# Loads of an attention decode kernel put in another order, and its MLP tail cut into chunks

## Chip, cores and metric

The kernel runs on one core of one Trainium2 chip. The metric is the device time of one execution in microseconds (us). Times in the profile count from the first instruction; the span in the profile is about 1.8 us shorter than the device time of the same run (731.0 and 732.81).

## The reference

The reference is one decode step of a transformer block for 8 sequences, with one new token each: adaptive layer norm, grouped-query attention over a cache of 8192 keys, and an MLP with a squared relu.

```python
mod = (silu(c) @ w_mod).reshape(8, 6, 1, -1)        # sa, ca, ga, sb, cb, gb
h = layernorm(x) * (1 + ca) + sa
q = (h @ wq)                                        # 32 query heads of 128
scores = einsum(q, k_cache) * 128 ** -0.5           # k_cache, v_cache: 8 x 8 heads x 8192 x 128, bf16
o = einsum(softmax(scores), v_cache)
x = x + ga * (o @ wo)
h = layernorm(x) * (1 + cb) + sb
r = relu(h @ w1 + b1)                               # 512 -> 1792
x = x + gb * ((r * r) @ w2 + b2)
```

The caches are 268 MB (2 x 8 x 8 x 8192 x 128 elements of 2 bytes), the weights about 15 MB. So the work is mostly reading.

## The kernel before

PE is the matmul engine, DVE, ACT and POOL are the vector, scalar and general engines, SP is the engine that issues the transfers, and SBUF is the memory on the core. There are 64 units, one for each sequence and KV head: a K load of 2 MB (2,097,152 bytes) and a V load of the same size. Unit u of K is transposed on PE, copied by DVE and multiplied with the queries. After the eight units of a sequence comes its softmax, and then its eight PV products, which are interleaved with the K units of the next sequence. Phase p therefore holds the K units of sequence p and the PV units of sequence p - 1. K has 4 slots in SBUF and V has 4. All loads are issued by one engine, SP, in program order, each after a wait for its slot.

```python
def k_unit(b, kvh, ...):
    ...
    if kn_use[ks] >= 1:
        W(SPq, S_ktfree[gbp], cntp)               # K slot: last transposed group copied out
    SPq(dma_start(Knat(ks), A_k_cache[b, kvh]...))
    ...
def v_unit(b, kvh):
    u = b * KVH + kvh
    vs = u % NVS
    ...
    if v_use[vs] >= 1:
        W(SPq, S_vfree[vs], v_use[vs])            # V slot: PV of unit u - 4 done
    SPq(dma_start(Vslot(vs), A_v_cache[b, kvh]...))
    ...                                            # 64 matmuls with 4 columns each
for ph in range(B + 1):
    for k in range(KVH):
        ...
        if ph < B:  k_unit(ph, k, ...)
        if ph >= 1:
            if ph == B and k == 4:
                epi_weights_a()                    # w1, w2 into K slots
                epi_weights_b()                    # wo into the transposed-K region, one transfer
            v_unit(ph - 1, k)
...
# the end: one wo product (32 matmuls), layer norm, then on [8, 1792] as a whole:
# w1 product -> + b1 (DVE) -> relu (ACT) -> square (DVE) -> 14 transposes -> copy -> w2 product -> + b2 (DVE)
```

## Time and profile before

| | before |
|---|---|
| device time, median of the first 4 runs | 732.29 us |
| mean load rate from 110 to 600 us | 425 GB/s |
| last V load usable on PE | 692.09 us |
| attention output (PV) done | about 694.0 us |
| wo product done | 703.9 us |
| output transfer issued | 729.31 us |

The page of the profile gives the span in 40 equal slices of 18.3 us. Each digit is a busy share in tenths (9 is 90% or more). DMA is the mean busy share of the core's 16 DMA engines, and the last line the rate in GB/s.

```profile
...
PE   3699898889889898989998988889888897640464
...
DMA  8999999999999999999999999999999999799600
GB/s 345 421 407 381 427 425 427 427 423 426 426 425 424 425 424 424 426 425 424 423 427 426 424 425 426 425 425 427 424 424 426 424 424 417 298 361 369 292 0 0
...
```

The rate is flat at 425 GB/s from slice 5 on. It dips in slice 4 (381), is low in slices 35 to 38, and is nothing in the last two. The table of windows shows the same in longer stretches: busy us of each engine (with its number of instructions), the granted clock, the DMA share and the rate.

```profile
...
core 0: us, PE busy (x) PEld busy (x) DVE busy (x) ACT busy (x) POOL busy (x), PEclk, DMA share, GB/s
50.00:65.00 15.00, 13.66 (x318) 12.78 (x315) 13.70 (x17) 0.00 (x0) 0.00 (x0) 1.00 0.95 354
110.00:600.00 490.00, 430.54 (x9524) 415.39 (x9521) 285.11 (x334) 65.39 (x390) 0.00 (x0) 0.79 1.01 425
616.00:640.00 24.00, 17.81 (x415) 16.79 (x416) 12.78 (x18) 2.10 (x13) 0.00 (x0) 0.78 0.83 326
640.00:694.00 54.00, 14.49 (x507) 13.91 (x504) 2.13 (x3) 8.79 (x54) 0.00 (x0) 0.50 0.90 342
...
```

In the long middle part the DMA engines are always busy (1.01) and PE is not (430.54 of 490 us). Share and rate are means over sixteen engines.

The list of waits (engine and line waiting, what it waited for; us in all, times, longest) shows what PE waits for at the end.

```profile
...
PE ps_ot L454 <- DMA Vb<-in_A_v_cache_dram: 33.5, 4, 24.5
...
```

The timeline (start, duration, engine, line, operation, output <- input, count) shows the end of the kernel.

```profile
...
653.21 15.28 SPq L442 DMA_DIRECT2D Vb<-in_A_v_cache_dram  x4
...
677.44 1.87 PE L454 MATMUL ps_ot<-PexpT,Vb 128*128 128x4 bf16 x64 [24.50 <-DMA Vb<-in_A_v_cache_dram]
...
692.09 1.87 PE L454 MATMUL ps_ot<-PexpT,Vb 128*128 128x4 bf16 x64 [2.99 <-DMA Vb<-in_A_v_cache_dram]
694.06 0.42 DVE L554 TENSOR_TENSOR OT_sb<-ps_ot,RB_sb 128x256 bf16<-128x256 f32 x1 [42.74 <-PE ps_ot L454]
...
694.54 9.35 PE L564 MATMUL ps_st<-KK,OT_sb 128*8 128x512 bf16 x32 [0.59 <-DVE OT_sb L554]
...
703.93 0.68 DVE L573 TENSOR_TENSOR ST_sb<-ps_st,mod_sb 8x512 f32<-8x512 f32 x1 [9.44 <-PE ps_st L564]
...
710.02 4.56 PE L610 MATMUL ps_kt<-KK,h2T 128*8 128x512 bf16 x16 [0.33 <-ACT h2T L591]
...
714.62 2.21 DVE L621 TENSOR_TENSOR KK<-ps_kt,b_sb 8x512 f32<-8x512 f32 x4 [5.25 <-PE ps_kt L610]
716.86 1.70 ACT L624 ACTIVATE KK<-KK 8x1792 f32<-8x1792 f32 x1 [6.89 <-DVE KK L621]
718.58 2.01 DVE L626 TENSOR_TENSOR Vb<-KK 8x1792 bf16<-8x1792 f32 x1 [1.76 <-ACT KK L624]
...
721.52 5.62 PE L648 MATMUL ps_st<-KK,r2T 128*8 128x512 bf16 x14 [0.34 <-ACT r2T L639]
...
729.31 0.31 SPq L665 DMA_DIRECT2D out_dram<-Vb  x1
```

The last four V loads (653.21, SP) reach PE from 677.44 to 692.09. Then follows a chain in which nothing overlaps and nothing is loaded: OT, the wo product 9.35, layer norm until 710.02, w1 product 4.56, bias 2.21, relu 1.70, square 2.01, w2 product 5.62. From the last V to the end it takes 39 us.

### The profile page before, as it was taken

Reading aid. Unit: us, or ns where it says so; the run is one execution under the profiler, and the core shown is the slowest. Engines: PE = TensorE matmul, PEld = TensorE weight load, DVE = VectorE, ACT = ScalarE, POOL = GpSimd, SP = SyncE. Lnnn points to the kernel's source line nnn. Section 1 sums busy time; section 2 is a strip of 40 time slices with the busy share of each in tenths; the row PEclk is TensorE's granted clock in tenths of the full one; section 3 lists DMA queues with packets and bytes.
Section 4 is the critical chain, followed back from the end, with each engine's and each line's share of the span. In section 5 each row is a group of like instructions: output and inputs, shape, how many; then the busy total and the mean of one; then the engine's idle time right before and its main releaser. Section 6 shows DMA issues by size and latency. Waiting matters only on the chain.

```text
span 731.0 us, 26450 instructions
## 1 busy us (share of the span) xinstructions
PE 581.6 (80%) x12560; PEld 540.9 (74%) x12560; DVE 384.7 (53%) x459; ACT 96.7 (13%) x535; POOL 2.0 (0%) x11
## 2 busy tenths in 40 slices
PE   3699898889889898989998988889888897640464
PEld 1688797879888798889987888789887897630321
DVE  0489665556565665556665554665555664510023
ACT  2000410005000500050003200050005000050001
POOL 0000000000000000000000000000000000000000
PEclk9799878768797877777778787876888878855567
DMA  8999999999999999999999999999999999799600
GB/s 345 421 407 381 427 425 427 427 423 426 426 425 424 425 424 424 426 425 424 423 427 426 424 425 426 425 425 427 424 424 426 424 424 417 298 361 369 292 0 0
DMA packets 26123, 285.39 MB, mean 390 GB/s; under 512 B 2168, under 2 KB 8088, under 8 KB 9120
## 3 DMA queue, kind: packets, MB, share of 16 engines
q1 hardware_dynamic: 26016, 283.71, 92.9%
q8 instruction: 98, 1.61, 0.9%
q14 instruction: 9, 0.07, 0.0%
HBM read 283.69 MB, written 0.01 MB: 388 GB/s over the span
## 4 chain that ended last, share of the span: by engine, by line
issue 94%; PE 3%; DMA 1%; DVE 1%; ACT 0%; SPq 0%; POOLq 0%; POOL 0%; ACTq 0%
DMA KK<-in_w_mod_dram 1%; PE ps_st L648 1%; PE ps_kt L610 1%; PE ps_kt L264 1%; PE ps_st L264 0%; DVE KK L621 0%; DVE Vb L626 0%; ACT KK L624 0%; DVE st L280 0%; DVE ST_sb L292 0%; DVE ST_sb L659 0%; DVE Vb L294 0%; DVE ST_sb L657 0%; DVE Vb L661 0%; POOLq L668 0%
## 5 line engine op out<-in xcount | busy, mean ns | idle before, releaser
L385 DVE COPY KK<-ps_kt 128x2048 bf16<-128x2048 bf16 x256 | 311.9, 1223 | 223.2 <-PE ps_kt L378 217.2
L378 PE MATMUL ps_kt<-ident,KK 128*128 128x128 bf16 x4096 | 350.1, 254 | 27.0 <-DMA KK<-in_A_k_cache_dram 17.1
L378 PEld LDWEIGHTS ps_kt<-ident,KK 128*128 128x128 bf16 x4096 | 303.0, 116 | 31.8 <-DMA KK<-in_A_k_cache_dram 18.7
L401 PE MATMUL ps_st<-QT,KK 128*128 128x4 bf16 x4096 | 146.7, 166 | 20.5 <-issue 12.1
L401 PEld LDWEIGHTS ps_st<-QT,KK 128*128 128x128 bf16 x4096 | 135.3, 100 | 34.7 <-DVE KK L385 20.0
L454 PE MATMUL ps_ot<-PexpT,Vb 128*128 128x4 bf16 x4096 | 119.6, 168 | 50.5 <-DMA Vb<-in_A_v_cache_dram 33.5
L454 PEld LDWEIGHTS ps_ot<-PexpT,Vb 128*128 128x128 bf16 x4096 | 114.2, 98 | 51.8 <-DMA Vb<-in_A_v_cache_dram 33.9
L490 ACT ACTIVATE PexpT<-ST_sb,NB_sb 128x64 bf16<-128x64 f32 x256 | 85.0, 333 | 0.2
L480 ACT COPY NB_sb<-ps_m 128x32 f32<-128x32 f32 x8 | 1.5, 185 | 529.4 <-PE ps_m L477 529.4
L490 ACT ACTIVATION_READ_ACCUMULATOR PexpT<-ST_sb,NB_sb 128x1 f32 x256 | 47.8, 187 | 0.0
L415 DVE COPY ST_sb<-ps_st 128x256 f32<-128x256 f32 x64 | 26.7, 417 | 16.8 <-PE ps_st L401 15.7
L417 DVE TENSOR_REDUCE pmax<-ST_sb 128x4 f32<-128x256 f32 x64 | 26.9, 420 | 2.2
L554 DVE TENSOR_TENSOR OT_sb<-ps_ot,RB_sb 128x256 bf16<-128x256 f32 x1 | 0.4, 425 | 42.7 <-PE ps_ot L454 42.7
L564 PE MATMUL ps_st<-KK,OT_sb 128*8 128x512 bf16 x32 | 9.3, 463 | 0.6 <-DVE OT_sb L554 0.6
L468 PE MATMUL ps_m<-ident,pmax_bf 128*32 128x128 bf16 x8 | 2.1, 264 | 9.5 <-DVE pmax_bf L465 9.5
L264 PE MATMUL ps_st<-KK,scT 128*8 128x512 bf16 x8 | 3.6, 628 | 7.6 <-DMA KK<-in_w_mod_dram 7.6
L280 DVE BATCH_NORM_STATS2 st<-x_sb 8x6 f32<-8x512 bf16 x1 | 0.7, 682 | 16.2 <-ACT mod_sb L271 16.2
L468 PEld LDWEIGHTS ps_m<-ident,pmax_bf 128*32 128x32 bf16 x8 | 0.8, 96 | 10.2 <-DVE pmax_bf L465 10.2
L591 ACT CAST h2T<-ps_m 128x32 bf16<-128x32 f32 x1 | 0.2, 185 | 61.0 <-PE ps_m L586 61.0
L564 PEld LDWEIGHTS ps_st<-KK,OT_sb 128*8 128x8 bf16 x32 | 3.3, 104 | 6.3 <-issue 3.2
L264 PEld LDWEIGHTS ps_st<-KK,scT 128*8 128x8 bf16 x8 | 0.9, 119 | 9.4 <-issue 9.4
L498 DVE CAST psr_hi<-psr 128x32 bf16<-128x32 f32 x8 | 1.4, 173 | 11.3 <-ACT PexpT L490 11.3
(67 smaller groups left out, 71.2 us busy)
## 6 DMA issues: line engine op xcount, KB each, us to landing
KK<-in_A_k_cache_dram SPq DMA_DIRECT2D x64, 2048.0 KB, 27.6
Vb<-in_A_v_cache_dram SPq DMA_DIRECT2D x64, 2048.0 KB, 31.0
Vb<-in_A_wq_dram SPq DMA_DIRECT2D x1, 4096.0 KB, 24.0
KK<-in_A_wo_dram SPq DMA_DIRECT2D x1, 4096.0 KB, 36.1
KK<-in_B_w_dram SPq DMA_DIRECT2D x2, 1792.0 KB, 22.5
KK<-in_w_mod_dram SPq DMA_DIRECT2D x1, 3072.0 KB, 10.2
b_sb<-in_B_b_dram SPq DMA_DIRECT2D x1, 28.0 KB
x_sb<-in_A_x_dram SPq DMA_DIRECT2D x1, 8.0 KB
```

Of the source, the lines that this page charges most:

```text
L264: mm = t.matmul(mod_bank(j), scT[:, kt, :], wmod_v[:, kt, j * CH:(j + 1) * CH], start=(kt == 0), stop=(kt == KT - 1))
L378: mm = t.matmul(kt_ps_tile(gb, j), Knat(ks)[:, tt, :], ident[:, :], is_transpose=True, start=True, stop=True)
L385: DVEq(lambda v, gb=gb, kts=kts, g=g: v.tensor_copy(KTs_grp(kts, g), kt_ps_grp(gb)).then_inc(S_ktfree[gb].h, 1))
L401: mm = t.matmul(ps_st[:, stb * 512 + tt * REP:stb * 512 + (tt + 1) * REP], KTs_tile(kts, tt), QT[:, b, kvh * REP:(kvh + 1) * REP], start=T ...
L415: DVEq(lambda v: v.tensor_copy(ST_sb[:, kvh, :, :], src).then_inc(P_dve.h, 1))
L417: DVEq(lambda v: v.tensor_reduce(pmax[:, kvh * REP:(kvh + 1) * REP], ST_sb[:, kvh, :, :], AX.X, ALU.max).then_inc(S_stfree[stb].h, 1))
L454: mm = t.matmul(ps_ot[:, col:col + REP], Vt(vs, tt), rhs, start=(tt == 0), stop=(tt == NT - 1))
L468: PEq(lambda t: t.matmul(ps_m[0:R, 0:P], pmax_bf[:, :], ident[:, :], start=True, stop=True).then_inc(P_pe.h, 1))
L490: ACTq(lambda a, kvh=kvh, h=h, r=r: a.activation(PexpT[:, pslot, kvh, h, :], ST_sb[:, kvh, h, :], ACT.Exp, bias=NB_sb[:, r:r + 1], scale=1 ...
L564: mm = t.matmul(AO_PS, lhsT, wo_v[:, Hh, :], start=(Hh == 0), stop=(Hh == HQ - 1))
L610: mm = t.matmul(mlp_bank(j, wdt), h2T[:, kt, :], w1_v[:, kt, n0:n0 + wdt], start=(kt == 0), stop=(kt == KT - 1))
L648: mm = t.matmul(Y_PS, r2T[:, kt, :], w2_v[:, kt, :], start=(kt == 0), stop=(kt == FT - 1))
```

## The change

The intent is to keep the load queue full and to overlap the end. It has five parts:

1. V0 to V3 are issued during phase 0, where until now only K was loaded.
2. The last four V units (60 to 63) go into K slots, which are free by then, so their loads need not wait for PV.
3. wo, w1 and w2 are loaded after all V, wo in eight pieces with a semaphore each; w1 and w2 go into V slots.
4. The biases are loaded as one row and added by a one-row matmul with ones at the end of each sum; relu, square, transposes and w2 product run in four chunks.
5. (1 + scale) of both layer norms is computed in the prologue.

```diff
+        def v_issue_early(u):                       # called for u = 0..3 after K4..K7 of phase 0
+            ...
+            SPq(dma_start(Vslot(u), A_v_cache[0, u]...))
         def v_unit(b, kvh):
+            tail = (b == B - 1) and (kvh >= KVH - NTAIL)
+            if not tail:
+                ...                                  # as before, or already issued early
+            else:
+                ks = u % NKN
+                W(SPq, S_ktfree[gbk], cntk)          # K slot of the same unit
+                SPq(dma_start(Knat(ks), A_v_cache[b, kvh]...))
...
-                    if ph == B and k == min(NVS, KVH - 1):
-                        epi_weights_a()
-                        epi_weights_b()
                     v_unit(ph - 1, k)
+        epi_weights()                               # wo in 8 pieces, then w1, w2
...
-        W(PEq, S_ldwo, ldwo)
+        for i in range(NWO):
+            W(PEq, S_ldwo[i], ldwo[i])
+            ...                                      # 4 of the 32 matmuls
...
+        for j, (n0, wdt) in enumerate(mlp_chunks):  # 512, 512, 512, 256 columns
+                for kt in range(KT):
+                    t.matmul(mlp_bank(j, wdt), h2T[:, kt, :], w1_v[:, kt, n0:n0 + wdt], start=(kt == 0), stop=False)
+                t.matmul(mlp_bank(j, wdt), ones_row, b1_sb[0:1, n0:n0 + wdt], start=False, stop=True)
...
+        for j, (n0, wdt) in enumerate(mlp_chunks):  # relu -> square -> transposes -> copy -> w2 product
```

## The prediction

> **What bounds the kernel now.** The memory stream does, until the epilogue. In the table of windows, 110 to 600 us runs at 425 GB/s with a DMA share of 1.01, while PE is 88% busy and waits little. One in-order SP queue loads everything (283.7 MB; 667 us at 425 GB/s), so slower stretches are time lost. The DMA packets in short windows show three:
>
> 1. 50 to 65 us: 355 GB/s. Phase 0 loads only K, into 4 slots, at 6.0 us of compute a unit; a 2 MB load takes 4.9 us. Loss about 2.6 us.
> 2. 616 to 640 us: about 320 GB/s, 5.7 us lost. The last V loads are let out one by one, every 10 us, as PV frees a slot (604.3 ... 634.9 us).
> 3. 635 to 692 us: w1, w2 and wo (7.9 MB, mostly 1 KB packets, 350 GB/s) go ahead of the last four V loads, whose issue waits for PV and then stands 13.8 us behind wo's descriptors. PE idles 24.5 us; the last V is used at 692.1.
>
> Then 37 us without any load: wo product 9.4, layer norm 6.1 to the next matmul, w1 product 4.6, bias 2.2, relu 1.7, square 2.0, transposes and copy 0.9, w2 product 5.6, three vector operations 2.1, output 1.7 (timeline).
>
> **What the change does.** V0 to V3 are issued during phase 0, which fills loss 1: -2.6 us, carried to the end by the memory bound. The last four V go into K slots, free since 633 us, so they are issued straight behind V59; wo (8 pieces with a semaphore each), w1 and w2 follow. Loss 2 stays: V56 to V59 still wait for PV in the same in-order queue. [...] the V waits hold back everything behind them.
>
> Tail, in the old clock, from V59's issue at 634.9:
> - data from 636.4; five V of 2.1 MB at 425 GB/s: until 661.1, last used about 663, PV done about 665 (was 694.0);
> - wo 4.2 MB at 350 GB/s: until 673.1, landed about 674.8; its matmuls keep pace with the pieces, done about 676 (was 703.9). The product is hidden, its load exposed;
> - layer norm less 0.45: w1 product starts 681.7. w1 lands about 679.5, w2 about 684.6: just in time;
> - w1 product with 4 bias rows (20 matmuls): 5.5, until 687.2;
> - relu, square, transposes and w2 in four chunks, partly overlapped: estimate 7.2 instead of 12.6, until 694.4 (6.2 to 8.3 by PE clock: 512-column matmuls show 0.21 and 0.43 us);
> - two vector operations 1.45, output 1.7: 697.5.
>
> Less the 2.6 of loss 1: a span of 695 (was 731.0), so a time of 696 us. By parts: tail order -27.8, MLP overlap and biases -5.3, phase 0 -2.6, layer norm -0.45. All is critical.
>
> **Prediction:** 696 us, 690 to 702 in 8 of 10. Faster by over 2%: 0.97; within 2%: 0.02; slower: 0.01.
>
> **What would show it:** 425 GB/s through 50 to 65 us; the dip at 615 to 640 still there; no PE gap of 24 us before a PV unit; last PV about 662, wo matmuls in groups waiting for DMA until 673, w1 product starting about 679 without a DMA wait.
>
> **What would make it wrong:** wo pieces slower than 350 GB/s; w1 or w2 landing late (a DMA wait before the w1 product); V early delaying K of phase 0 so that PE work is lost later; chunk hand-overs dearer than 0.1 us each.

What the trace shows is the order of issue: SP waited 79.3 us for PV (56 times, longest 10.3), V56 to V59 were issued at 604.3, 614.9, 625.1 and 635.0, and w1, w2 and wo only after them, at 635.3, 635.8 and 636.4. "Data from 636.4" can be seen in the packets: there the 16 KB packets under way at one time go from 8 to 14. The 13.8 us are the length of V60's issue (653.21 to 667.0); that wo's descriptors held it up is my reading.

## The result

| | before | after |
|---|---|---|
| device time, median (range) | 732.77 us (731.78 to 734.58, 12 runs) | 707.04 us (704.64 to 709.41, 9 runs) |
| ratio of the mean times, 95% interval | | 0.9644 (0.9628 to 0.966) |
| span of the profiled run | 731.0 us | 705.9 us |

A ratio here is the mean time of one kernel's fast runs over that of the other's of the same rounds, so it is not quite the ratio of the medians quoted. The kernel became 3.6% faster, clear of noise. The forecast of 696 us, with 690 to 702 as its range, was missed by 11 us: about 26 us were gained where 36 were expected.

The slices of the page after (17.6 us each):

```profile
...
PE   3699699888889889888988898997988798893667
...
DMA  8999999999999999999999999999999999989990
GB/s 345 426 425 426 425 426 424 425 424 424 397 425 428 422 419 421 426 426 425 424 426 422 424 425 423 424 426 425 425 424 423 427 424 425 403 329 371 397 336 4
...
```

The dip of slice 4 is gone (426), and PE works through the slices in which it stood still. A small dip is new in slice 11 (397); the closer reading below returns to it. The windows, with columns as before:

```profile
...
50.00:65.00 15.00, 14.02 (x319) 12.83 (x316) 13.94 (x16) 0.00 (x0) 0.00 (x0) 1.00 1.01 426
110.00:600.00 490.00, 432.11 (x9591) 416.35 (x9589) 285.83 (x334) 65.75 (x390) 0.00 (x0) 0.78 1.01 424
616.00:640.00 24.00, 19.53 (x422) 18.77 (x419) 12.41 (x16) 0.00 (x0) 0.00 (x0) 0.75 0.79 303
640.00:690.00 50.00, 28.01 (x558) 18.25 (x559) 7.26 (x15) 11.45 (x67) 0.54 (x1) 0.60 0.97 368
...
```

From 50 to 65 us the rate rose from 354 to 426 GB/s, as predicted. From 616 to 640 us the dip is still there, also as predicted (303 GB/s). PE's wait for V is now

```profile
...
PE ps_ot L491 <- DMA KK<-in_A_v_cache_dram: 3.8, 2, 3.6
...
```

instead of 33.5 us. The end of the kernel in the timeline after:

```profile
...
668.22 1.87 PE L491 MATMUL ps_ot<-PexpT,KK 128*128 128x4 bf16 x64 [3.60 <-DMA KK<-in_A_v_cache_dram]
...
670.68 7.84 PE L602 MATMUL ps_st<-KK,OT_sb 128*8 128x512 bf16 x24 [0.59 <-DVE OT_sb L591]
...
680.44 1.04 PE L602 MATMUL ps_st<-KK,OT_sb 128*8 128x512 bf16 x4 [0.47 <-DMA KK<-in_A_wo_dram]
681.51 0.68 DVE L612 TENSOR_TENSOR ST_sb<-ps_st,mod_sb 8x512 f32<-8x512 f32 x1 [10.89 <-PE ps_st L602]
...
687.28 1.87 PE L653 MATMUL ps_kt<-Vb,h2T 128*8 128x512 bf16 x4 [0.33 <-ACT h2T L630]
...
689.08 0.58 PE L654 MATMUL ps_kt<-b_sb,ones_bf 1*8 1x512 bf16 x1
...
694.22 1.02 PE L653 MATMUL ps_kt<-Vb,h2T 128*8 128x256 bf16 x4
...
695.47 0.26 PE L674 MATMUL ps_m<-ident,Vb 8*128 8x8 bf16 x4
...
702.30 0.37 PE L688 MATMUL ps_st<-b_sb,ones_bf 1*8 1x512 bf16 x1
...
704.13 0.32 SPq L703 DMA_DIRECT2D out_dram<-Vb  x1
```

The last V is used at 668.22. The first 24 matmuls of the wo product then run in one go, since their six pieces are there in time. The other eight wait briefly for the last two pieces (0.41 and 0.47 us), and the product ends at 681.5. The w1 product starts at 687.28, without a wait for DMA. In it a group of four 512-column matmuls takes 1.87 us (the last group, of 256 columns, 1.02) and a 512-column bias matmul 0.58 us; the transposes that follow it start at 695.47. Set beside the sum of the prediction (its times less the 2.6 us for phase 0):

| term | predicted | measured | off by |
|---|---|---|---|
| last V usable on PE | 660.4 | 668.2 | +7.8 |
| from there to the end of the wo product | 13.0 | 13.3 | +0.3 |
| layer norm, to the w1 product | 5.7 | 5.8 | +0.1 |
| w1 product with biases | 5.5 | 8.2 | +2.7 |
| relu to the w2 product, in chunks | 7.2 | 7.2 | 0.0 |
| two vector operations and output | 3.15 | 3.2 | 0.0 |
| span | 695 | 705.9 | +11 |

Two terms carry the whole error. The rest of the sum held to half a microsecond. For the last but one row that is partly luck: the relu and the square of the first chunk had already run beside the long w1 product (the relu at 689.70), while the clock record was still at 0.5 for the first 3.9 of the 7.2 us (until 699.4). The experiments are about the two terms that failed.

### A closer reading: sixteen landings for each load

The kernel takes a load as finished when its semaphore has received sixteen increments, and the trace holds the time of each (256 for the sixteen loads of a K slot). I take them for one from each of the sixteen DMA engines: sixteen 16 KB packets of 0.61 us are under way at a time (15 to 17 from 300 to 310 us, in both kernels). The records do not name the engine of a packet or of an increment. Sorted by time, this is what the increments say (here, as in the counts of packets, from the raw records of the trace, not a view of the profile; us):

```
              before                              after
load   first   8th    9th    last       first   8th    9th    last
K0      16.0   16.4   16.4   16.6        16.1   16.3   16.3   16.7
K24    224.6  226.0  229.5  231.9       224.2  224.8  226.3  228.4
K48    459.6  462.5  470.7  474.4       459.5  461.3  468.7  470.9
V55    611.2  615.0  626.9  630.9       611.1  613.0  624.9  627.2
V58    632.6  633.0  642.7  646.0       635.8  636.0  639.8  642.2
V59    642.6  643.0  648.0  651.0       645.0  645.4  645.6  647.4
V63    688.2  688.9  688.9  692.0       664.6  665.4  665.8  668.2
```

The landings fall into two groups of eight, which I take for two groups of DMA engines. One group runs ahead, and the other falls back steadily: at V55 the ninth landing comes 11.9 us after the eighth, and the last one 16 to 20 us after the first. A load counts only when the last has landed: V63's last landing is at 692.0 and 668.2, its first PV matmul at 692.09 and 668.22. The dip of the mean rate at 616 to 640 us is the group ahead, which has used up its queue: in the kernel before, 7 or 8 packets are under way from 632.4 to 636.0 us instead of 16. e3 tests this. The group behind never pauses: before, the last landings from V55 to V59 follow each other every 4.8 to 5.3 us (630.9, 635.8, 641.1, 646.0, 651.0), and after likewise (627.2, 632.0, 637.3, 642.2, 647.4). The new dip of slice 11 is of the same kind: there the lag of the late group (mean of the last eight landings less mean of the first eight) shrinks from 3.6 us (K18) to 2.2 (K20), and the last landings stay 3.5 us ahead of the old ones (K22: 208.8 against 212.3). Not every run with the early V loads has it (382 in e3, none in e8), and what starts it was not tested.

So the prediction's step "data from 636.4; five V of 2.1 MB at 425 GB/s: until 661.1, last used about 663" started with V59 from an empty queue. The queue was empty for half of the engines only, as the 8 packets under way show. Even in the kernel before, V59 landed last at 651.0, and four more loads at 5 us each give 671, not 663.

Theory S: the slower group of DMA engines sets the time of every load, and it is slower because these eight also fetch the instructions of PE (98 packets of 16,384 bytes in a queue of their own). The rival, theory C, takes the engines as alike and puts the delay on the issue: the early V loads delayed the K loads of phase 0 (K8 landed last at 88.4 instead of 70.7), units then ended 3 to 8 us later to the end, and V59 was issued at 637.9 instead of 634.9.

### The profile page after: what moved, and what is told of

The parts are those of the page before. It is cut to its first block, busy times and chain, and to the rows that moved or that the text cites. A ratio compares the mean times of both kernels' runs of the same rounds, so it can differ in the third digit from the quotient of the medians.

```text
span 705.9 us, 26469 instructions
## 1 busy us (share of the span) xinstructions
PE 588.4 (83%) x12565; PEld 543.0 (77%) x12565; DVE 382.6 (54%) x457; ACT 97.8 (14%) x541; POOL 2.0 (0%) x11
## 3 DMA queue, kind: packets, MB, share of 16 engines
q8 instruction: 98, 1.61, 0.9%
## 4 chain that ended last, share of the span: by engine, by line
issue 94%; PE 3%; DMA 1%; DVE 1%; ACT 0%; SPq 0%; POOLq 0%; POOL 0%; ACTq 0%
DMA KK<-in_w_mod_dram 1%; PE ps_kt L653 1%; PE ps_st L686 1%; PE ps_kt L268 1%; PE ps_st L268 1%; PE ps_kt L654 0%; ACT r2T L679 0%; PE ps_m L674 0%; DVE ST_sb L294 0%; DVE ST_sb L697 0%; DVE Vb L296 0%; DVE Vb L699 0%; DVE st L284 0%; POOLq L706 0%; ACT mod_sb L275 0%
## 5 line engine op out<-in xcount | busy, mean ns | idle before, releaser
L385 PE MATMUL ps_kt<-ident,KK 128*128 128x128 bf16 x4096 | 353.9, 255 | 21.7 <-issue 16.7
L491 PE MATMUL ps_ot<-PexpT,Vb 128*128 128x4 bf16 x3840 | 112.5, 168 | 19.9 <-issue 18.0
L491 PEld LDWEIGHTS ps_ot<-PexpT,Vb 128*128 128x128 bf16 x3840 | 107.3, 97 | 21.1 <-issue 21.1
L528 ACT ACTIVATION_READ_ACCUMULATOR PexpT<-ST_sb,NB_sb 128x1 f32 x256 | 50.9, 199 | 0.0
L491 PE MATMUL ps_ot<-PexpT,KK 128*128 128x4 bf16 x256 | 7.5, 168 | 6.5 <-DMA KK<-in_A_v_cache_dram 3.8
L491 PEld LDWEIGHTS ps_ot<-PexpT,KK 128*128 128x128 bf16 x256 | 7.2, 103 | 6.7 <-DMA KK<-in_A_v_cache_dram 4.0
L668 DVE TENSOR_TENSOR Vb<-Vb 8x512 bf16<-8x512 f32 (+1 forms) x4 | 2.4, 612 | 11.9 <-ACT Vb L666 11.9
## 6 DMA issues: line engine op xcount, KB each, us to landing
KK<-in_w_mod_dram SPq DMA_DIRECT2D x1, 3072.0 KB, 10.3
```

Source lines behind the costliest of these rows:

```text
L385: mm = t.matmul(kt_ps_tile(gb, j), Knat(ks)[:, tt, :], ident[:, :], is_transpose=True, start=True, stop=True)
L491: mm = t.matmul(ps_ot[:, col:col + REP], tile(tt), rhs, start=(tt == 0), stop=(tt == NT - 1))
L528: ACTq(lambda a, kvh=kvh, h=h, r=r: a.activation(PexpT[:, pslot, kvh, h, :], ST_sb[:, kvh, h, :], ACT.Exp, bias=NB_sb[:, r:r + 1], scale=1 ...
```

## Experiments

"Before" in this section means the runs of the kernel before on the same chip in the same job. For each kernel I give its median, its ratio and the landing or duration that decides.

### e1: without the early V loads

```diff
-                    if ph == 0 and 4 <= k < 4 + 4:
-                        v_issue_early(k - 4)
```

> The changed kernel without the early V loads; all else kept. Theory S (the slowest DMA engines set every landing and never idle; early V brings all landings 3.5 us forward and that is kept to the end): V63 lands about 3.5 us later, time about 710. Theory C (early V put compute 3 us behind the kernel before, V59 is issued at 637.9 instead of 634.9 and that is carried to the end): V59 issued about 635, time about 702 to 704.

Measured: 707.98 us (706.6 to 710.66, 4 runs), ratio 0.9656 (0.963 to 0.9682). V63's last landing came at 670.2 instead of 668.2. V59 was issued earlier, as theory C wants, but its last landing was later (649.6 against 647.4). So theory C is refuted: an earlier issue bought nothing. Theory S has the sign of the landing right, with 2.0 us instead of 3.5 (a landing of a single trace is good to about 1 us: V55 landed last at 629.6 here and at 630.9 in the kernel before, with the same loads up to it); in the times the difference from the changed kernel (0.9656 against 0.9644) is within the noise.

### e2: the early V loads alone, in the kernel before

```diff
+                    if ph == 0 and 4 <= k < 4 + 4:
+                        v_issue_early(k - 4)          # and v_unit takes them as issued
```

> The kernel before with the early V loads alone. Theory S: all landings 3.5 us earlier to the last V, time about 729. Theory C: unit ends 3 to 5 us later in phase 7 and 8, time 735 to 737.

Measured: 730.75 us (4 runs) with 733.91 before, ratio 0.9959 (0.9944 to 0.9975), so 3 us faster, clear of noise. V55 landed last at 627.5 instead of 630.9, V63 at 689.9 instead of 692.0. This is theory S, and it confirms the prediction's first term (2.6 us).

### e3: V60 to V63 issued in pairs with V56 to V59

```diff
-                    v_unit(ph - 1, k)
+                    v_unit(ph - 1, k if ph < B else (k // 2 + (k % 2) * 4))
```

> The changed kernel with V60 to V63 each issued (and used) right behind V56 to V59, as their K slots come free, so that the queue is never short at 616 to 640 us. Theory S: the mean rate there rises to 425 GB/s, but only on the engines that are ahead; the last landing of the last V stays within 1 us, time 705 to 708. If the dip of the mean rate was time lost (as the prediction had it), the last V lands 4 to 6 us earlier and the time is about 701.

Measured: 705.52 us (703.32 to 707.62, 4 runs), ratio 0.9626 (0.9593 to 0.9659). The window of the dip now reads

```profile
...
616.00:640.00 24.00, 20.11 (x443) 19.35 (x439) 12.75 (x18) 0.00 (x0) 0.00 (x0) 0.76 1.00 423
...
```

423 GB/s at a share of 1.00 where the changed kernel has 303 and 0.79: the dip is filled. And V63's last landing is at 667.7, against 668.2. Its first landing moved from 664.6 to 650.6. All that the fuller queue gained went to the landings that were ahead. The dip, counted in the prediction as "5.7 us lost", was not a loss.

### e4: two V units loaded by sixteen 8-partition transfers

```diff
+                    if u in (16, 40):
+                        for p0 in range(0, P, 8):
+                            SPq(dma_start(Vslot(vs)[p0:p0 + 8], A_v_cache[b, kvh]...[p0:p0 + 8]).then_inc(S_v[vs].h, 16))
```

> The changed kernel with two V units (16 and 40) loaded by sixteen 8-partition transfers instead of one of 128. If such transfers run on eight engines alone: theory S says that eight engines are behind because they also fetch instructions. If the eight used are those ahead, the spread between first and last landing of V55 falls from 16 us to under 8 and the last V lands 6 to 8 us earlier, time about 699. If they are those behind, the spread grows to 30 us or more and the time to 713 or more. If all engines are alike (theory C), no such change of the spread, time 706 to 709.

Measured: 743.24 us (738.12 to 745.51, 4 runs), ratio 1.0123: 36 us slower than the changed kernel. The experiment failed as a test. For each such transfer the trace has nine semaphore updates, one at once and eight as data landed, which I take for eight engines, but its 16 KB packets took about 1.0 to 1.5 us where they otherwise take 0.61, and the rate fell to 221 GB/s for a slice. After it, the sorted landings show neither "all those ahead" nor "all those behind" displaced: of the eight late ones, six keep their distance from then on and two fall back further, so the eight used seem to be a mixture. Why the packets are slow was not tested.

### e5: fewer PE instructions, same loads

```diff
-                for tt in range(NT):
+                for tt in range(0, NT, 8):              # wrong result on purpose
...                                                     # and the stop flag on the last of them
```

> The changed kernel with PV on one V tile in eight: wrong result on purpose, same loads, 7168 fewer PE instructions (28 of the 98 instruction fetches of 16 KB). Theory S (eight of the sixteen DMA engines are late because they also fetch the PE's instructions, about 1.4 us each fetch): spread of V55's landings falls from 16 us to about 11.5, the last landing of V63 from 668.2 to about 663, first landings unchanged. If those engines are slow for another reason, spread and landing stay (16 us, 668).

Measured: 698.35 us (2 runs), ratio 0.9527. (The comparison passed all the same, because attention adds little to the output within its tolerance; the kernel is still wrong.) V63's last landing: 661.7, where theory S expected about 663. The queue that carries the instructions, in the list of DMA queues (packets, MB, share of sixteen engines' span), for the changed kernel:

```profile
...
q8 instruction: 98, 1.61, 0.9%
...
```

and for this one:

```profile
...
q8 instruction: 70, 1.15, 0.7%
...
```

The 28 packets less for 7168 instructions less mean 64 bytes an instruction, so these packets are PE's instructions. The distance between the eighth and the ninth landing of V55 fell from 11.9 to 8.6 us (611.9 and 620.5), and the spread from first to last only to 14.6 us, not to the 11.5 that I had expected. These two are poor measures, since the group ahead lost some of its lead at slice 11 in the changed kernel and not here. The lag of the late group from K24 to V55, where every slice up to 599 us is at 419 GB/s or more, is cleaner (raw records; the first landings of the two loads are 386 to 387 us apart in all three):

| | PE fetches in that stretch | lag at K24, at V55 | growth | growth for each fetch, times eight engines |
|---|---|---|---|---|
| before | 61 | 5.07, 16.21 us | 11.14 us | 1.46 us |
| changed kernel | 62 | 3.25, 14.09 us | 10.84 us | 1.40 us |
| e5 | 42 | 4.95, 12.34 us | 7.39 us | 1.41 us |

In the same time the lag grew by a third less with a third fewer fetches, and for each fetch by the same. Had these engines been slow for a reason apart from the fetches, I would expect the lag to grow with the time. (In the other kernels told of here, e4 and e6 apart, it is 1.31 to 1.45.) And between 624.2 and 660.4 us e5 fetches no PE instruction: from V59 to V63 the lag stands still (9.26 and 9.24 us). So my estimate is that a fetch holds its engine up by about 1.4 us, as expected (the last column, which shares the fetches evenly among eight engines), although its packet lasts only 1.06 us in the records; what the rest is stays open. This kernel also issues its late loads earlier (V59 at 624.8), because PE has less to do, but e1 and e3 show that an earlier issue does not bring the last landing forward.

### e6: more instructions on an idle engine, same loads and PE work

```diff
+        for i in range(5120):
+            g.memset(pool_scr[...one element...], 0.0)     # POOL
```

> The changed kernel with 5120 one-element memsets added on the idle POOL engine: [...] same loads and PE work. Theory S: the engines that fetch them fall back by about 1.4 us per fetch; if they are the same eight, V63's last landing is 3 to 4 us later (about 672) and the time about 711; if they are others, the spread narrows and the time stays. If fetches do not matter: spread and landing as before (16 us, 668).

Measured: 718.89 us (2 runs), ratio 0.9807, so 12 us slower than the changed kernel. V63's last landing: 675.8, 7.6 us later. The queues of instructions:

```profile
...
q8 instruction: 98, 1.61, 0.9%
q14 instruction: 49, 0.40, 0.1%
...
```

PE's fetches are the same 98. The new ones come on another queue, 40 packets of 8 KB (49 in place of 9). By the landings they did not spread over eight engines. At V55 seven landings are still ahead (609.8 to 610.9), eight lie where the late group of the changed kernel has them (625.0 to 627.2), and one is alone behind all (634.4, 24.6 us after the first instead of 16). I take this for one engine of the group ahead that has become the last because it carries the new fetches. Its lag behind the seven grew from 5.7 us (K16) to 24.1 (V55). Of the 12 us, 7.6 are this landing. Another 3 to 4 us are a flaw of the experiment: the layer norm's power on POOL had to wait for the last memset (694.88), so the w1 product started 9.2 us after the wo product instead of 5.8. The size was not as expected (3 to 4 us), but the kind is plain: 0.33 MB of instructions, 0.1% of the traffic, moved the landing of the last V by 7.6 us.

### e7, e12, e13: bias rows padded to 128 rows of zeros

The second term is the w1 product: 8.2 us instead of 5.5. Its matmuls all ran at the half clock (clock record 0.5 from 685.8 to 699.4 us). The bias matmuls of the kernel have one row (1*8 and 1x512 in the timeline); here they have 128, of which 127 are zeros. The clock records last whole multiples of 3.41 us (98 records before, 96 after, all but the last of each); these steps are what the expectations call windows.

```diff
-        b1_sb = sb("b1_sb", [1, F], BF16)
+        b1_sb = sb("b1_sb", [P, F], BF16)             # zeroed by POOL, row 0 loaded
-        ones_row = ones_bf[0:1, 0:B]
+        ones_row = ones_bf[:, 0:B]
...                                                     # b2 likewise
```

> The changed kernel with the bias rows padded to 128 rows of zeros, so that the bias matmuls use all rows of the array; same count and columns. If one-row matmuls keep PE at the half clock: [...] takes 5.5 to 6.5 us instead of 8.2; time about 704.5. If the clock's windows or the mere count of 20 matmuls are the cause: 8 us still, time unchanged at 706 to 708.

(A clause about when the full clock comes is cut, since no run had shown it; what "takes 5.5 to 6.5 us" is the w1 product.)

> The 128-row bias kernel of e7 unedited, for a second profile and more times. If one-row matmuls are what keeps the half clock (w1 product 8.1 to 8.2 us in four of seven profiles of one-row kernels so far, 6.2 to 7.3 in the others): 6.0 to 6.9 us again and a median of about 704.5 with a scatter under 3 us. If it is the phase of the windows alone: a w1 product of 7 to 8.2 is as likely as for one row, times scattered over 5 us around 706.

> A third look at the 128-row bias kernel, with the same expectations as the second: 6.0 to 6.9 us if the rows matter, 7 to 8.2 us at least once in three looks if only the phase does.

Measured: 703.92, 703.57 and 703.55 us, ratios 0.9609, 0.9599 and 0.9604 (the last 0.9585 to 0.9624), with 13 runs of which 11 lie between 703.0 and 704.6. The w1 product took 6.12, 6.08 and 5.58 us. The first of them, in the timeline:

```profile
...
686.36 1.87 PE L656 MATMUL ps_kt<-Vb,h2T 128*8 128x512 bf16 x4 [0.33 <-ACT h2T L633]
...
688.02 0.63 PE L657 MATMUL ps_kt<-b_sb,ones_bf 128*8 128x512 bf16 x1
...
692.48 0.25 PE L677 MATMUL ps_m<-ident,Vb 8*128 8x8 bf16 x4
...
```

The seven profiles of kernels with one-row bias matmuls (the changed kernel twice, e1, e3, e4, e5, e6) show 8.19, 8.08, 8.19, 6.20, 7.05, 7.26 and 8.19 us. The clock records fit this: with one row, the full clock came 3.6 to 15.2 us after the w1 product began, in four of seven over 7 us; with 128 rows it came after 3.5 to 4.6 us, three times of three. But the rows alone do not decide it, since in e3 the product took 6.20 us with one row

```profile
...
686.20 1.87 PE L653 MATMUL ps_kt<-Vb,h2T 128*8 128x512 bf16 x4 [0.33 <-ACT h2T L630]
688.00 0.58 PE L654 MATMUL ps_kt<-b_sb,ones_bf 1*8 1x512 bf16 x1
...
692.20 0.27 PE L654 MATMUL ps_kt<-b_sb,ones_bf 1*8 1x256 bf16 x1
692.40 0.25 PE L674 MATMUL ps_m<-ident,Vb 8*128 8x8 bf16 x4
...
```

while with one-row matmuls a late full clock was the more frequent case. The times show that the rows cost some 3 us; that they do it by way of the clock rests on ten profiles. The scatter of the changed kernel, 704.6 to 709.4 us in 9 runs, fits this, as do e3's four runs, which fall into two pairs (703.3 and 703.7, 707.4 and 707.6); but only one run of each job has a profile, so the link of time and clock is argued here and not shown run by run.

### e8: the bias rows first, in the time of the layer norm

```diff
+        def _pe_bias(t):                              # right after the wo product
+            for j, (n0, wdt) in enumerate(mlp_chunks):
+                t.matmul(kt_bank_f32(j, B, 0, wdt), ones_row, b1_sb[0:1, n0:n0 + wdt], start=True, stop=False)
+            t.matmul(Y_PS, ones_row, b2_sb[0:1, :], start=True, stop=False)
...                                                   # w1 and w2 products add to these sums
```

> The changed kernel with the bias rows multiplied first, during the layer norm, where PE has nothing to do (start of each sum), so the w1 product is 16 full matmuls again: 4.6 to 5.5 us instead of 8.2, and 0.4 less at the end. Time about 703.5. If the half clock stays for another reason: w1 product 6.9 us, time about 705.5.

Measured: 703.52 us (702.7 to 703.92, 4 runs), ratio 0.9596 (0.9571 to 0.9621). The bias matmuls now run at 681.04, in idle time, and the w1 product is 5.60 us long (686.91 to the transposes at 692.51):

```profile
...
681.04 0.92 PE L615 MATMUL ps_kt<-b_sb,ones_bf 1*8 1x512 bf16 x4
...
686.91 5.67 PE L666 MATMUL ps_kt<-Vb,h2T 128*8 128x512 bf16 x16 [0.33 <-ACT h2T L643]
692.51 0.25 PE L687 MATMUL ps_m<-ident,Vb 8*128 8x8 bf16 x4
...
```

### e9, e10, e11: a better version

e9 is the changed kernel again. e10 joins e3 and e8. e11 adds twelve idle matmuls during the layer norm, to see whether the full clock then lasts until the w1 product.

```diff
+            for i in range(12):                       # e11 only
+                t.matmul(ps_ot[0:B, 0:512], OT_sb..., wo_v[:, HQ - 1, :], start=True, stop=True)
```

> The changed kernel once more, unedited, so that the next two are compared with it on the same chip and in the same job. Both theories: about 707, with a scatter of some 5 us[...]; the last landing of V63 at 668 again, with 8 DMA engines late.

> The changed kernel with V60 to V63 paired with V56 to V59 (e3) and the bias rows first (e8). V63 lands last at 667.5 to 668; w1 product 5.6; time about 702.5, scatter under 3 us.

> As the run before it, plus 12 idle 512-column matmuls on PE during the layer norm[...]. If the clock's window is what makes the w1 product 5.6 instead of 3.5: w1 product 3.5 to 3.9, time about 700.5. If the clock falls all the same, no change, or 1 to 2 us lost where the idle matmuls run at the half clock.

| | median us (range, runs) | ratio to before | w1 product us | last landing of V63 |
|---|---|---|---|---|
| e9 | 707.08 (705.45 to 708.39, 5) | 0.9646 | 8.08 | 667.8 |
| e10 | 702.09 (701.76 to 702.43, 4) | 0.9578 (0.9558 to 0.9598) | 5.50 | 667.5 |
| e11 | 701.43 (700.09 to 701.84, 5) | 0.9567 (0.9547 to 0.9586) | 4.81 | 667.3 |

e9 repeats the result: 707 us, a V63 at 668, a w1 product of 8.1. e10 is 5 us faster than it (702.09 / 707.08 = 0.993) and scatters by 0.7 us instead of 3. e11's idle matmuls

```profile
...
681.14 2.76 PE L618 MATMUL ps_ot<-KK,OT_sb 128*8 128x512 bf16 x12
...
685.94 4.87 PE L666 MATMUL ps_kt<-Vb,h2T 128*8 128x512 bf16 x16 [0.33 <-ACT h2T L643]
690.75 0.25 PE L687 MATMUL ps_m<-ident,Vb 8*128 8x8 bf16 x4
...
```

ended at 683.9; the clock fell to half at 687.0 all the same and came back at 690.4. The w1 product was 0.7 us shorter than in e10, not the 1.6 to 2.0 hoped for. The gain of e11 over e10 is within the noise. e10 and e11 both beat the kernel before and the changed kernel.

## Why the prediction was wrong, and where it was right

- **"The memory stream does"** bound the kernel: right, and confirmed by e1, e2 and e3, but read too coarsely. What binds is not 425 GB/s on average but the slower eight of sixteen DMA engines, as I read the 11.9 us between the eighth and the ninth landing of V55.
- **Loss 1, phase 0**: right. The rate rose to 426 GB/s and the last landings came 3.5 us earlier (K48: 474.4 to 470.9; V55: 630.9 to 627.2), e2 measured 3 us. The feared side effect, K delayed and compute late, happened (K8 17.7 us later, V59 issued 3.0 us later) and cost nothing, because V59's slowest part was still in the queue.
- **Loss 2, "about 320 GB/s, 5.7 us lost"**: wrong. The dip was there after the change, as foretold, but it was not a loss. e3 filled it to 423 GB/s, and V63's last landing moved by 0.5 us.
- **The step that failed: "data from 636.4; five V of 2.1 MB at 425 GB/s: until 661.1, last used about 663"**. The last V was usable at 668.2 in a clock where that term reads 660.4: 7.8 of the 11 us. The step took the mean rate for the pace of every engine and the dip for an empty queue; eight engines were some 12 to 16 us behind at V55, each PE instruction fetch costing one of them about 1.4 us by the estimate in e5, and they never paused (a last landing every 4.8 to 5.3 us from V55 to V59; e3). The landing of V59 at 651.0 in the old trace would have shown it.
- **"w1 product with 4 bias rows (20 matmuls): 5.5"**: mis-sized; it took 8.2, the other 2.7 us. The scheme of chunks and bias rows was right, but the count of matmuls was taken over at the old mixture of clocks. With one-row matmuls the full clock came after 3.6 to 15.2 us (seven profiles), with all rows after 3.5 to 4.6 (three), and the product took 5.6 to 6.1 us (e7, e12, e13).
- **Everything else of the sum was right**: the order of the tail (wo keeps pace with its pieces, 13.3 us against 13.0), layer norm 5.8 against 5.7, the chunked MLP 7.2 against 7.2 (partly luck, see above), no DMA wait before the w1 product, no long PE gap before PV.
- **Where the 25.1 us of span came from**: the last load of the kernel ended hardly earlier (692.0 before, 689.9 after, now w2 in place of V63). What shrank is the part after it, from 39.0 to 16.0 us, because PV, wo product and layer norm now run beside loads. 2.1 and 23.0 are the 25.1.

- **Left open**: which eight engines fetch the instructions (the records do not name a packet's engine), why a fetch costs its engine 1.4 us when its packet lasts 1.06, the 2 us of spread inside each group at V55, and why the 8-partition transfers of e4 are slow. Whether a loop in place of the unrolled instructions would help was not tried.

## What to carry to other kernels

In this kernel a load was as late as the last of its sixteen landings (V55: first 611.1, last 627.2 us), so read the last landing (and the distance from the first) before turning a dip of the mean rate into lost time: here the dip was the faster engines waiting (8 packets under way instead of 16) while the slower ones never stopped, and filling it moved the last landing by 0.5 us (e3). The unrolled instruction stream was itself DMA traffic (98 packets, 1.61 MB for PE); as I read the landings, it fell on some engines only, and every load paid for it (e5: 28 packets less, V63 lands 6.5 us earlier). One-row matmuls in a short burst between idle times cost more here than their columns (about 3 us, e7); in e8 they ran where PE waits anyway, and the time was 703.5 us instead of 707.
